# Attention with two MLPs in float32 products: the query/key high copies move from ScalarE to GpSimd, and every third two-block high copy of the transposed weights moves from ScalarE to VectorE

## Chip, core and metric

One core of a Trainium2 chip. The time is device microseconds (us) of one execution. Engines are named as the profile names them: PE is TensorE (PEld its weight loads), DVE is VectorE, ACT is ScalarE, POOL is GpSimd, SP issues the DMAs.

## What is computed

```python
scores = scale * np.matmul(q, k.transpose(0, 1, 3, 2))      # (4, 8, 576, 576), head_dim 64
thresh = np.max(scores, axis=-1, keepdims=True) - tau
scores = np.where(scores >= thresh, scores, -1000000000.0)
attn = softmax(scores)
x = np.matmul(attn, v)                                      # heads side by side: (2304, 512)
x = (silu(x @ w_gate) * (x @ w_val)) @ w_out                # first MLP, d_ff 1536
x = relu(x @ w_in) ** 2 @ w_out2                            # second MLP, d_ff 2048
```

## The kernel before

Products are made in a reduced-width float32 format (fp32r). A value that needs more width is kept as two tiles, a high copy (the value rounded to fp32r) and a low copy (the value less its high copy), and a product of two such values takes three matmuls. A **high copy** is one instruction that copies, a **low copy** one that subtracts.

**Phase 1, attention (to about 445 us).** 16 pairs of heads, four pairs in each of four batches, nine tiles of 128 query rows per pair: 144 tiles. The loop over tiles calls these steps, which the names below refer to:

- `QK` (L615): score matmuls into one of two score buffers `s`.
- `RED` (L625, DVE): the row maximum less tau. `CUT` (L633, ACT): scores below it are pushed out, into the single buffer `z`. `EXP` (L641, ACT): into one of three buffers `e`, with the row sum.
- `RCP` (L646, DVE): the reciprocal of the row sum. `NORM` (L651, POOL): `e` is scaled by it.
- `TR` (L670, PE): two tiles later, `e` is transposed in five 128-column blocks, three into one PSUM bank (the three-block half, 128x384) and two into another (the two-block half, 128x256). From tile 20 on there are only these two banks, used alternately, so each half of a tile waits until the same half of the tile before has been read out.
- `PH` (L690, ACT): the high copies of the two halves into `pt`. `PL` (L61 writing `pt`, DVE): the low copies, which read the bank again and the high copy; with the second read the bank is free for the next `TR`.
- `AV` (L716; L713 in batch 0): attention times values into `xF`, through a DMA `pt<-pt` on SP (L701) that moves a tail of 64 rows.

In batch 0 the weights are kept whole instead of split: one half is copied by ACT and the other by DVE (`ways` K and E, L53 and L55, writing `x`), and AV takes one matmul per block (L713). In batches 1 to 3 every tile is of `way` V: both high copies by ACT, both low copies by DVE.

**Preparing the next pair** (`pair_steps`, called one step at a time in the tile loop for pairs 1 to 15): the raw queries and keys, 128x576 each, get high copies into `land` (queries L560 on ACT with the scale, keys L53 on ACT), then the low copy of the queries on DVE (L566) and that of the keys on POOL (L61 writing `raw`, two halves); twelve DMAs on SP spread them over the two heads' tiles `qs`, `kh`, `kl`; POOL makes `qt` and the values' copies `vs`.

**The loader.** Until about 180 us weights for the first MLP are converted from the 64-bit words of the input, in 128x256 pieces: ACT L137, four DVE instructions (L139, L141, L145, L147), a high copy on ACT, a low copy on POOL (L61 writing `wa`, `wx`).

**The fill.** From the end of batch 0 the first MLP's first group (five of twelve d_ff blocks, L226, L271) is run for six half batches in between, as work for PE while attention waits for other engines. **Phase 2**, from 445 us, is the rest of the MLPs.

**What sets the order.** The code is written tile by tile, and each step carries a priority offset (`CFG["early"]`). A scheduler that knows the engines and a cost per instruction sets each engine's queue from that; a queue then runs strictly in order on the chip. So moving an instruction to another engine changes the order of others as well.

Of the kernel before, what the change touches and what calls it, by code (L numbers as in the profile page):

```python
# [14 lines left out]
AF = mybir.ActivationFunctionType  # L15
# [4 lines left out]
P = 128  # L20
B, H, S, D = 4, 8, 576, 64
# [46 lines left out]
def attention_moe(tc, qkv, qk0, tau, w1, w2, out, cfg):  # L68
    nc = tc.nc
    ops = Ops(nc)  # L70
# [525 lines left out]
    pt = ptp.tile([P, 10, 640], F32R, name="pt", tag="pt")  # L596
# [56 lines left out]

    WAYS = {"V": "VV", "F": "AA", "E": "AD", "K": "DA", "D": "DD"}

    def way(t):
        b, p, i = tiles[t]
        return WAYS[cfg["way"][b % len(cfg["way"])][i]]  # L660

# [18 lines left out]
    def halves(t):  # L680

        return ((st[t]["tx"], 0, 3, way(t)[0]), (st[t]["ty"], 3, 2, way(t)[1]))

    def PH(t):
        o = PTCOL[tiles[t][2]]
        for src, s0, n, how in halves(t):
            if how in "AD":
                ops.copy(how, ptf[:, s0 : s0 + n, o : o + P], src)
                continue
            nc.scalar.activation(pt[:, s0 : s0 + n, o : o + P], src, AF.Copy)  # L690

    def PL(t):
        o = PTCOL[tiles[t][2]]
# [139 lines left out]
    for i in range(NTILE + lag + 1):  # L833
# [11 lines left out]
        if 0 <= t < NTILE:  # L845
            at_(PH, t)
# [164 lines left out]
def pack(inputs):  # L1011
# [38 lines left out]


CFG = {
    "kh": "A",
    "kl": "P",
    "vh": "P",
    "vl": "P",
    "way": ("KEKKEKKEK", "VVVVVVVVV", "VVVVVVVVV", "VVVVVVVVV"),
    "lag": 2,
    "xh": "AAAA",
    "xl": "DDDD",  # L1060
    "u1": ("P", "P"),
    "u2": ("A", "D"),
    "qs": "A",
    "zs": 1,
    "wl": "PD",
    "live": (3, 2),
# [18 lines left out]
def program(arrays):  # L1085
    import concourse.bacc as bacc

    nc = bacc.Bacc("TRN2", target_bir_lowering=False, num_devices=1, dynamic_dma_scratch_size=1024)
    args = [nc.dram_tensor(n, a.shape, mybir.dt.from_np(a.dtype), kind="ExternalInput").ap() for n, a in arrays]
    out = nc.dram_tensor("out_0_dram", (NT, DM), F32, kind="ExternalOutput").ap()  # L1090
    with tile.TileContext(nc) as tc:
        attention_moe(tc, *args, out, CFG)
    return nc
# [9 lines left out]
```

## Time and profile before

| | us |
|---|---|
| median of 3 runs | 1168.59 |
| the three runs | 1168.59, 1168.98, 1165.98 |
| the profiled execution | 1168.51 |
| its span, first to last instruction | 1166.7 |
| granted TensorE clock, mean | 0.998 of full speed |

The profile page gives each engine's busy time over the span. PE is busy 97% of it, DVE 71%, ACT 57%, POOL 21%, but these are averages over phase 1, where four engines share each tile, and phase 2, where PE alone is full. A PE row's duration holds the pipeline's latency, so that rows overlap and a busy PE can still lose time: what PE loses is read better from how many matmuls it starts in a stretch.

### The profile page before, as it was taken

The numbers are of one execution on the slowest core, as the hardware profiler recorded it, in microseconds if no ns is written. First come the engines' busy times: TensorE is split into PE (matmuls) and PEld (weight loads), VectorE is DVE, ScalarE is ACT, GpSimd is POOL, SyncE is SP. The second block draws the span as 40 slices with busy tenths as digits, with TensorE's granted clock in tenths as the row PEclk, the third lists the DMA queues.
The fourth block names the chain that finished last, engine by engine and source line by source line (L and its number), as shares of the span: only waits on it lengthen the run. The fifth ranks groups of instructions, "written<-read, shape, count | busy, mean of one in ns | idle before, by whom it ended". The sixth has DMA issues, their size and how long they took to land.

```text
span 1166.7 us, 19455 instructions
## 1 busy us (share of the span) xinstructions
PE 1128.8 (97%) x6444; PEld 993.8 (85%) x6444; DVE 832.6 (71%) x2042; ACT 667.7 (57%) x1570; POOL 250.7 (21%) x397
## 2 busy tenths in 40 slices
PE   6888999999999999999999999999999999999998
PEld 5667889899999999998888888888888888888887
DVE  6988997877787773988976854478458758755433
ACT  6888988988888872554433422255455435433321
POOL 5556664656554531000000000000000000000000
PEclk9999999999999999999999999999999999999999
DMA  6775554555454510332210210002102101100111
GB/s 195 192 212 158 154 126 115 121 120 140 114 127 116 127 23 20 92 99 81 82 46 28 81 37 1 1 28 82 37 19 77 50 19 46 46 1 1 46 61 58
DMA packets 52053, 92.70 MB, mean 79 GB/s; under 512 B 8176, under 2 KB 16368, under 8 KB 51952
## 3 DMA queue, kind: packets, MB, share of 16 engines
q1 hardware_dynamic: 51808, 91.45, 28.4%
q8 instruction: 51, 0.84, 0.3%
q14 instruction: 50, 0.41, 0.1%
q10 hardware_dynamic: 144, 0.00, 0.0%
HBM read 51.91 MB, written 4.72 MB: 49 GB/s over the span
## 4 chain that ended last, share of the span: by engine, by line
PE 77%; DVE 8%; ACT 5%; DMA 4%; issue 3%; POOL 1%; SPq 0%; POOLq 0%; ACTq 0%; DVEq 0%
PE mm L226 34%; PE mm L317 17%; PE mm L271 9%; PE bank L226 5%; PE bank L670 3%; PE bank L716 3%; PE bank L271 3%; PE s L615 2%; DMA pt<-pt 2%; DVE st__101 L625 2%; DVE pt L61 2%; ACT z L633 1%; ACT e L641 1%; ACT pt L690 1%; PE bank L713 1%
## 5 line engine op out<-in xcount | busy, mean ns | idle before, releaser
L226 PE MATMUL mm<-xs,wa 128*128 128x512 f32 (+2 forms) x1152 | 226.3, 356 | 0.5 <-ACT x L53 0.5
L226 PEld LDWEIGHTS mm<-xs,wa 128*128 128x128 f32 x1152 | 193.5, 188 | 30.9 <-ACT x L53 0.7
L226 PE MATMUL mm<-xs,wb 128*128 128x512 f32 (+1 forms) x840 | 175.5, 368 | 0.0
L670 PE MATMUL bank<-ident,e 128*128 128x128 f32 x720 | 158.5, 278 | 16.8 <-DVE pt L61 5.3
L226 PEld LDWEIGHTS mm<-xs,wb 128*128 128x128 f32 x840 | 146.8, 189 | 26.3
L651 POOL TENSOR_SCALAR e<-e,r 128x576 f32<-128x576 f32 x144 | 112.8, 783 | 131.0 <-DVE r L646 89.0
L61 DVE TENSOR_TENSOR pt<-bank,pt 128x384 fp32r<-128x384 f32 x216 | 100.3, 486 | 43.1 <-ACT pt L690 41.2
L625 DVE TENSOR_SCALAR_CACHE_REDUCE st__101<-s,tau_c 128x576 bf16<-128x576 f32 x144 | 116.7, 810 | 7.7 <-PE s L615 6.7
L633 ACT ACTIVATE z<-s,thr 128x576 f32<-128x576 f32 x144 | 106.8, 741 | 25.3 <-DVE st__101 L625 19.1
L670 PEld LDWEIGHTS bank<-ident,e 128*128 128x128 f32 x720 | 94.9, 142 | 30.4 <-POOL e L651 9.3
L300 ACT ACTIVATE k_th<-mm 128x512 f32<-128x512 f32 (+1 forms) x80 | 43.7, 546 | 121.3 <-PE mm L226 120.1
L226 PE MATMUL bank<-xs_m,wa 128*128 128x288 f32 x576 | 107.6, 323 | 2.9 <-DVE xs_m L61 2.2
L641 ACT ACTIVATE e<-z 128x577 f32<-128x577 f32 x144 | 99.6, 692 | 1.7
L690 ACT ACTIVATE pt<-bank 128x384 fp32r<-128x384 f32 x216 | 87.9, 437 | 19.1 <-PE bank L670 18.2
L226 PEld LDWEIGHTS bank<-xs_m,wa 128*128 128x128 f32 x576 | 87.9, 189 | 6.4 <-DVE xs_m L61 3.6
L615 PE MATMUL s<-kh,qs 128*128 128x288 f32 x256 | 79.8, 324 | 9.3 <-DVE qs L500 5.9
L301 DVE TENSOR_TENSOR k_th<-k_th 128x512 f32<-128x512 f32 (+1 forms) x80 | 50.8, 635 | 53.1 <-ACT k_th L300 52.6
L716 PE MATMUL bank<-pt,vs 128*128 128x256 f32 (+1 forms) x432 | 84.3, 318 | 1.5 <-DMA pt<-pt 1.3
L137 ACT ACTIVATE wf<-wr 128x256 f32<-128x256 f32 x106 | 45.6, 433 | 69.6 <-DMA wr<-in_w_dram 57.9
L330 DVE TENSOR_TENSOR xF<-xF,mm 128x512 f32<-128x512 f32 x54 | 37.0, 685 | 54.7 <-PE mm L317 54.7
L615 PE MATMUL s<-kl,qs 128*128 128x288 f32 x256 | 74.5, 304 | 0.0
L716 PEld LDWEIGHTS bank<-pt,vs 128*128 128x128 f32 x432 | 66.5, 189 | 2.8 <-issue 2.4
(120 smaller groups left out, 2136.6 us busy)
## 6 DMA issues: line engine op xcount, KB each, us to landing
wr<-in_w_dram SPq DMA_DIRECT2D x106, 256.0 KB, 2.9
raw<-in_qkv_dram SPq DMA_DIRECT2D x15, 896.0 KB, 5.1
kh<-land SPq DMA_DIRECT2D x60, 144.0 KB, 2.5
kl<-raw SPq DMA_DIRECT2D x60, 144.0 KB, 2.6
xF<-in_w_dram SPq DMA_DIRECT2D x30, 256.0 KB, 3.2
kd<-kl SPq DMA_DIRECT2D x32, 144.0 KB, 2.4
out_dram<-xF SPq DMA_DIRECT2D x18, 256.0 KB, 2.0
qs<-land SPq DMA_DIRECT2D x30, 144.0 KB, 2.4
```

The source lines that it names most:

```text
L61: e.tensor_tensor(out, a, b, op=ALU.subtract)
L226: mm(pt[:, :n], w[:, a, col + c * P : col + (c + 1) * P], xs[:, b, c, :], start=(i == 0), stop=(i == len(TERMS) - 1),)
L271: mm(pt[:, :n], w[:, a, 2 * DM + m * P : 2 * DM + (m + 1) * P], u[:, b, :], start=(k == 0), stop=(k == last),)
L317: mm(pt, u[:, b, s * P : (s + 1) * P], w[:, a, DM : 2 * DM], start=(k == 0), stop=(k == last),)
L615: mm(sp[:, cols], l, r[:, cols], start=(n_ == 0), stop=(n_ == len(pairs) - 1),)
L625: red = nc.vector.tensor_scalar(st_, st[t]["s"][:, :S], scalar1=tau_c, scalar2=None, op0=ALU.subtract, op1=ALU.max, accum_out=th)
L633: nc.scalar.activation(z[:, :S], st[t]["s"][:, :S], AF.Prelu, bias=st[t]["thr"], scale=-1.0, alpha=1 / SLOPE)
L641: ex = nc.scalar.activation(e, st[t]["z"], AF.Exp, scale=-SLOPE, accum_out=sum_)
L651: nc.gpsimd.tensor_scalar(e, e, scalar1=r, scalar2=1.0, op0=ALU.mult, op1=ALU.mult)
L670: mm(dst[:, j], e[:, c0 : c0 + P], ident, is_transpose=True, start=(j == 0), stop=(j == len(cols) - 1),)
L690: nc.scalar.activation(pt[:, s0 : s0 + n, o : o + P], src, AF.Copy)
L716: mm(o[:, :n], hd["vs"][:, SLOT[k % 5], :], pt[:, k, lo : lo + n], start=(k == 0), stop=(k == 9))
```

## The change

`CFG["kh"]` and `CFG["qs"]` go from A to P: in `pair_steps` both high copies into `land` (L560 and L53 before) are made by POOL, for the 15 pairs that go through it. A new way H is VV with the difference that `PH` makes the two-block half's high copy on DVE; in batches 1 to 3 the tiles 2, 5 and 8 of each pair's nine are of way H, 36 of 108 tiles. Low copies, DMAs and the arithmetic stay.

```diff
-    WAYS = {"V": "VV", "F": "AA", "E": "AD", "K": "DA", "D": "DD"}
+    WAYS = {"V": "VV", "H": "VH", "F": "AA", "E": "AD", "K": "DA", "D": "DD"}
...
             if how in "AD":
                 ops.copy(how, ptf[:, s0 : s0 + n, o : o + P], src)
                 continue
-            nc.scalar.activation(pt[:, s0 : s0 + n, o : o + P], src, AF.Copy)
+            ops.copy("D" if how == "H" else "A", pt[:, s0 : s0 + n, o : o + P], src)
...
 CFG = {
-    "kh": "A",
+    "kh": "P",
...
-    "way": ("KEKKEKKEK", "VVVVVVVVV", "VVVVVVVVV", "VVVVVVVVV"),
+    "way": ("KEKKEKKEK", "VVHVVHVVH", "VVHVVHVVH", "VVHVVHVVH"),
...
-    "qs": "A",
+    "qs": "P",
```

In the built program POOL has 30 more instructions that write `land` (15 of L562, 15 of L57), ACT 30 fewer and 36 fewer that write `pt` (216 to 180), and DVE 36 new ones (L55 CAST writing `pt`). The scheduler has moved others with them. Three places follow, before and then after in each.

The queue of POOL at the end of batch 0, where pair 4 is prepared; `e0_97` and `e1_98` with `r30` and `r31` are the NORMs of tiles 30 and 31. Before:

```order
L651 TENSOR_SCALAR e0_97<-e0_97,r30_1023 128x576
L61 TENSOR_TENSOR vs8_1156<-raw4_982,vs8_1156 128x5x64
L57 TENSOR_SCALAR vs9_1231<-raw4_982 128x5x64
L61 TENSOR_TENSOR wa_69<-xF_64,wa_69 128x256
L61 TENSOR_TENSOR vs9_1231<-raw4_982,vs9_1231 128x5x64
L61 TENSOR_TENSOR raw4_982<-raw4_982,land4_984 128x288 x2
L57 TENSOR_SCALAR qt02_117<-qs8_1123 64x64
L61 TENSOR_TENSOR wx_73<-wf2_80,wx_73 128x256
L651 TENSOR_SCALAR e1_98<-e1_98,r31_1052 128x576
```

After:

```order
L651 TENSOR_SCALAR e0_97<-e0_97,r30_1023 128x576
L562 TENSOR_SCALAR land4_984<-raw4_982,qscale_59 128x576
L57 TENSOR_SCALAR land4_984<-raw4_982 128x576
L57 TENSOR_SCALAR vs8_1156<-raw4_982 128x5x64
L61 TENSOR_TENSOR raw4_982<-raw4_982,land4_984 128x288 x2
L61 TENSOR_TENSOR vs8_1156<-raw4_982,vs8_1156 128x5x64
L57 TENSOR_SCALAR vs9_1231<-raw4_982 128x5x64
L61 TENSOR_TENSOR wa_69<-xF_64,wa_69 128x256
L61 TENSOR_TENSOR vs9_1231<-raw4_982,vs9_1231 128x5x64
L61 TENSOR_TENSOR wa_69<-xF_64,wa_69 128x256
L651 TENSOR_SCALAR e1_98<-e1_98,r31_1052 128x576
```

The two `land` copies stand in the block between the two NORMs, which goes from eight instructions to ten; a `qt` copy and a piece of `wx` have moved behind it, and the first `vs8` copy and a piece of `wa` into it.

The queue of DVE in batch 1, pair 1, while the loader still runs, from the RED of tile 52 (`thr52`); `pt` written from `bank0` and `bank1` are the two PLs of a tile, `xs_m01` splits the next fill's input. Before:

```order
L625 TENSOR_SCALAR st__101,thr52_1926<-s0_108,tau_c_60 128x576
L728 TENSOR_TENSOR xF_64<-xF_64,bank3_87 64x256
L646 RECIPROCAL r51_1940<-sum51_1887 128x1
L61 TENSOR_TENSOR pt_131<-bank0_84,pt_131 128x3x128
L256 SCALAR_TENSOR_TENSOR m00_4_th_1813<-m00_4_th_1813,bank2_86 128x288
L61 TENSOR_TENSOR pt_131<-bank1_85,pt_131 128x2x128
L61 TENSOR_TENSOR xs_m01_1948<-xF_64,xs_m01_1948 128x288
```

After:

```order
L625 TENSOR_SCALAR st__101,thr52_1926<-s0_108,tau_c_60 128x576
L147 SCALAR_TENSOR_TENSOR xF_64<-xF_64 128x256
L728 TENSOR_TENSOR xF_64<-xF_64,bank3_87 64x256
L256 SCALAR_TENSOR_TENSOR m00_4_th_1813<-m00_4_th_1813,bank2_86 128x288
L141 TENSOR_SCALAR xF_64<-xF_64 128x256
L566 SCALAR_TENSOR_TENSOR raw6_1727<-raw6_1727,qscale_59,land6_1729 128x576
L145 SCALAR_TENSOR_TENSOR xF_64<-xF_64 128x256
L61 TENSOR_TENSOR xs_m01_1948<-xF_64,xs_m01_1948 128x288 x2
L646 RECIPROCAL r51_1940<-sum51_1887 128x1
L61 TENSOR_TENSOR xs_m01_1948<-xF_64,xs_m01_1948 128x288 x2
L61 TENSOR_TENSOR pt_131<-bank0_84,pt_131 128x3x128
L61 TENSOR_TENSOR pt_131<-bank1_85,pt_131 128x2x128
```

The tile's two PLs stood third and fifth behind the RED; now they stand behind ten other instructions, among them L566, three of the loader and all four of `xs_m01`.

The queue of DVE in batch 2, after the loader's end, from the RED of tile 106. Before:

```order
L625 TENSOR_SCALAR st__101,thr106_4213<-s0_108,tau_c_60 128x576
L728 TENSOR_TENSOR xF_64<-xF_64,bank3_87 64x256
L646 RECIPROCAL r105_4224<-sum105_4179 128x1
L61 TENSOR_TENSOR pt_131<-bank0_84,pt_131 128x3x128
L61 TENSOR_TENSOR pt_131<-bank1_85,pt_131 128x2x128
L625 TENSOR_SCALAR st__101,thr107_4265<-s1_109,tau_c_60 128x576
L646 RECIPROCAL r106_4275<-sum106_4218 128x1
L61 TENSOR_TENSOR pt_131<-bank0_84,pt_131 128x3x128
L61 TENSOR_TENSOR pt_131<-bank1_85,pt_131 128x2x128
L625 TENSOR_SCALAR st__101,thr108_4300<-s0_108,tau_c_60 128x576
```

After:

```order
L625 TENSOR_SCALAR st__101,thr106_4213<-s0_108,tau_c_60 128x576
L728 TENSOR_TENSOR xF_64<-xF_64,bank3_87 64x256
L646 RECIPROCAL r105_4224<-sum105_4179 128x1
L61 TENSOR_TENSOR pt_131<-bank0_84,pt_131 128x3x128
L61 TENSOR_TENSOR pt_131<-bank1_85,pt_131 128x2x128
L646 RECIPROCAL r106_4275<-sum106_4218 128x1
L625 TENSOR_SCALAR st__101,thr107_4265<-s1_109,tau_c_60 128x576
L55 CAST pt_131<-bank1_85 128x2x128
L61 TENSOR_TENSOR pt_131<-bank0_84,pt_131 128x3x128
L61 TENSOR_TENSOR pt_131<-bank1_85,pt_131 128x2x128
L625 TENSOR_SCALAR st__101,thr108_4300<-s0_108,tau_c_60 128x576
```

The CAST of an H tile stands directly in front of that tile's two PLs, and the RCP has changed places with the RED.

## Rows read from the trace of the kernel before

**Rows 1.** Windows by stage: length, busy us and instructions per engine, clock, DMA.

```profile
8.00:60.00 52.00, 43.72 (x233) 35.83 (x232) 44.48 (x120) 44.54 (x108) 29.13 (x46) 1.00 0.72 195
60.00:128.00 68.00, 59.53 (x359) 50.01 (x358) 59.43 (x162) 60.95 (x151) 43.20 (x62) 0.97 0.63 174
128.00:180.00 52.00, 47.80 (x348) 44.65 (x348) 48.99 (x127) 45.43 (x116) 33.35 (x51) 1.00 0.53 134
180.00:300.00 120.00, 115.97 (x861) 109.99 (x860) 94.55 (x258) 103.50 (x260) 66.58 (x107) 1.00 0.52 124
300.00:445.00 145.00, 142.74 (x1083) 138.76 (x1082) 109.77 (x298) 121.67 (x306) 70.01 (x110) 1.00 0.41 97
445.00:1166.70 721.70, 716.91 (x3565) 612.58 (x3564) 472.57 (x1073) 288.72 (x632) 4.65 (x8) 1.00 0.14 46
```

**Rows 2.** Windows, the fullest 20 us of batch 3: columns as in Rows 1.

```profile
420.00:440.00 20.00, 19.95 (x155) 19.71 (x155) 12.04 (x34) 14.17 (x37) 5.24 (x8) 1.00 0.06 13
```

**Rows 3.** Waits, 180 to 445 us: who waited for whom, us, times, longest.

```profile
POOL e L651 <- DVE r L646: 54.8, 38, 3.0
DVE pt L61 <- ACT pt L690: 39.6, 67, 1.2
...
PE bank L670 <- DVE pt L61: 2.3, 6, 0.7
```

**Rows 4.** Timeline around 157 us: start, us, engine, line, operation, idle before.

```profile
154.00 1.57 POOL L61 TENSOR_TENSOR raw<-raw,land 128x288 fp32r<-128x288 f32 x2
154.52 1.34 DVE L145 SCALAR_TENSOR_TENSOR xF<-xF 128x256 int32<-128x256 int32 x1
155.78 0.84 DVE L139 TENSOR_SCALAR wf<-wf 128x256 f32<-128x256 f32 x1
157.60 0.30 PE L670 MATMUL bank<-ident,e 128*128 128x128 f32 x1 [1.26 <-DVE pt L61]
```

**Rows 5.** Timeline around 229 us: columns as in Rows 4.

```profile
228.30 0.50 ACT L690 ACTIVATE pt<-bank 128x384 fp32r<-128x384 f32 x1
228.82 0.22 ACT L53 ACTIVATE xF<-bank 64x64 f32<-64x64 f32 x1
229.05 0.38 ACT L690 ACTIVATE pt<-bank 128x256 fp32r<-128x256 f32 x1
229.63 0.52 PE L670 MATMUL bank<-ident,e 128*128 128x128 f32 x3 [0.65 <-DVE pt L61]
```

**Rows 6.** Tile raw: duration ns min/median/max, first and last start us, forms.

```profile
L514 POOL TENSOR_SCALAR qs<-raw,qscale x1: 744/744/744, 7.3 to 7.3; 128x576 fp32r<-128x576 f32 x1
L57 POOL TENSOR_SCALAR vs<-raw x24: 452/458/1044, 91.7 to 407.4; 128x320 fp32r<-128x320 f32 x24
L560 ACT ACTIVATE land<-raw,qscale x15: 760/777/820, 16.5 to 390.5; 128x576 fp32r<-128x576 f32 x15
L566 DVE SCALAR_TENSOR_TENSOR raw<-raw,qscale,land x15: 796/820/1435, 17.3 to 391.4; 128x576 fp32r<-128x576 f32 x15
L53 ACT ACTIVATE land<-raw x15: 665/682/705, 17.8 to 391.2; 128x576 fp32r<-128x576 f32 x15
```

**Rows 7.** Groups by form, ACT and DVE, 180 to 445 us: busy, mean ns, idle before.

```profile
L690 ACT ACTIVATE pt<-bank 128x256 fp32r<-128x256 f32 x89 | 34.3, 386 | 0.8 <-PE bank L670 0.7
L61 DVE TENSOR_TENSOR pt<-bank,pt 128x384 fp32r<-128x384 f32 x88 | 48.8, 554 | 33.6 <-ACT pt L690 32.4
```

**Rows 8.** Groups by form, DVE, 8 to 128 us: columns as in Rows 7.

```profile
L55 DVE COPY x<-bank 128x256 f32<-128x256 f32 x12 | 5.0, 420 | 2.6 <-PE bank L670 2.5
```

**Rows 9.** Groups by form, DVE L145, 128 to 180 us: columns as in Rows 7.

```profile
L145 DVE SCALAR_TENSOR_TENSOR xF<-xF 128x256 int32<-128x256 int32 x5 | 3.5, 709 | 0.0
```

**Rows 10.** Groups by form, DVE L145, 445 us to the end: columns as in Rows 7.

```profile
L145 DVE SCALAR_TENSOR_TENSOR wf<-wr,wf 128x256 int32<-128x256 int32 x106 | 44.6, 421 | 1.5
```

**Rows 11.** Timeline of POOL and PE at the end of batch 0: columns as in Rows 4.

```profile
97.24 1.97 POOL L61 TENSOR_TENSOR raw<-raw,land 128x288 fp32r<-128x288 f32 x2
...
100.10 0.74 POOL L651 TENSOR_SCALAR e<-e,r 128x576 f32<-128x576 f32 x1
100.89 0.76 PE L670 MATMUL bank<-ident,e 128*128 128x128 f32 x5 [1.68 <-POOL e L651]
```

## The prediction, made before the changed kernel ran

> **What bounds the kernel now.** I read the windows by stage first. From 445 us on PE is busy 716.9 of 721.7 us and ACT 288.7: nothing that the change touches is left to be late there, so that only the first 445 us can move, and they move the end one for one [rows 1]. In them I ask how much PE loses, because the matmuls are the same in both kernels. Busy time hides it, so I count starts: in the fullest stretch PE starts 155 matmuls in 20 us, 129 ns each [rows 2]. At that rate the 348 of 128 to 180 us need 44.9 of 52 us, the 861 of 180 to 300 us need 111.1 of 120, and the 1083 of 300 to 445 us need 139.7 of 145 [rows 1]. PE loses some 7.1, 8.9 and 5.3 us there, 21 us in all. (The mix of matmuls differs a little between stretches; I give each loss an error of 1 us.) Before 128 us there is no fill to run and PE is not the bound at all: ACT is busy 105.5 and DVE 103.9 of 120 us.
>
> Then the waits, to see who makes PE lose that. The two-bank turn of the transposes is the place: PE waits for DVE's low copy, which waits for ACT's high copy, 39.6 us in 67 waits after 180 us [rows 3]. Two samples tell the stages apart. Near 157 us PE sits idle 1.26 us for a low copy that DVE reaches late because the loader's instructions stand ahead of it; one of them took 1.34 us, with POOL subtracting beside it [rows 4]. That is DVE's lateness: it is busy 49.0 of 52 us there [rows 1]. Near 229 us PE sits idle 0.65 us, and ACT has been copying without a break, with two pieces of `xF` work between and behind the two high copies [rows 5]. That is ACT's lateness.
>
> **What the change takes and adds.** ACT loses 15 query copies of 777 ns and 15 key copies of 682 ns [rows 6], 21.9 us, and 36 two-block copies of 386 ns [rows 7], 13.9 us: 35.8 us in all. DVE gains 36 copies out of PSUM of that shape. No row of before has it writing `pt`, but the same engine copies the same 128x256 out of a bank into `x` in 420 ns [rows 8]: 15.1 us. POOL gains 30 copies of 128x576. The one such copy with the scale took 744 ns, and 458 ns for 320 columns would make at most 824 for 576 [rows 6]. I take 770 ns, nearest the first because it is the same shape: 23.1 us, with 22.3 and 24.7 as ends.
>
> *Up to 128 us.* Five pairs are prepared there, so ACT loses 5 x 1.46 = 7.3 us. If ACT alone set the pace the whole of it would come off, and if DVE did, nothing; they are equally busy, and each tile passes through both in turn, so I take a quarter, -1.8 us. Against it stand two prices on POOL's side. First, an instruction of DVE that reads SBUF takes longer beside POOL: the loader's L145 took 709 ns at 128 to 180 us and 421 after POOL had fallen silent [rows 9, 10], L566 between 796 and 1435 [rows 6]. POOL, busy 72.3 of 120 us, gets 7.7 us more, about a tenth. If a loader instruction is stretched by 0.29 us where POOL works six tenths of the time, a tenth more of POOL's time stretches some 100 of them by 0.03 to 0.05 us: 3 to 5 us of DVE work at most, of which I put 0.8 on the path, since only part of DVE's queue is waited for. Second, POOL's queue is in order, and the two copies stand ahead of a NORM at the end of batch 0. There the block is already late: two subtractions of 1.97 us, then NORM, and PE idle 1.68 us for it [rows 11]. Two copies are 1.54 us more in that block, less a `qt` and a `wx` that have left it, plus a `vs` and a `wa` that have come in. I take +0.5, with 0 and +1.5 as ends. Sum -0.5, between -5 (most of ACT's time comes off) and +3.
>
> *128 to 180 us.* Six H tiles fall here: 6 x 0.42 = 2.5 us on an engine that has 3 us to spare in 52 [rows 1], so that it would be busy 99%. ACT's relief (2.9 + 2.3 us) is not what this stage waits for. The new order adds to it: in the second place shown, the two low copies of a tile stand behind the loader, L566 and all of `xs_m01`, some 4 us of DVE later than before, though the order gives PE a dozen more fill matmuls there first (about 1.6 us). I take +2, between 0 (the casts replace waits for ACT) and +4.
>
> *180 to 445 us.* ACT is busy 225.2 of 265 us, 85%; eight pairs and 29 casts take 11.7 + 11.2 = 22.9 us off, and it falls to 76%. DVE goes from 204.3 us to 216.5, 77% to 82%. The casts have a cover: DVE sits idle 33.6 us ahead of the three-block low copy [rows 7], and in the third place shown a cast stands just there, so that ACT copies one half while DVE copies the other. Without that cover they cost up to 12.2 us. POOL waits 54.8 us for reciprocals before its NORMs [rows 3], and no wait of PE for POOL is among the large ones here, so 12.3 us more on POOL cost nothing; without that slack each pair would pay up to 1.5 us. Of the 14.2 us that PE loses here, part is the wait for `pt<-pt` transfers and for the fill's own split, which ACT's relief hardly touches. I call half of it, 7 us, ACT's lateness, and take half of that off, -3.5, since only one two-block copy in three is moved and the three-block one, on which DVE waits most, stays on ACT. New lateness of DVE gives back 1. Sum -2.5, between -7 and +3.
>
> In all -0.5 + 2 - 2.5 = -1.0 us. The profiled execution took 1168.51 us, 1.8 more than its span and the same as the median to 0.1 us, so the forecast is 1167.5 us.
>
> [...]
>
> **The rivals.** *Relief goes through.* If ACT's order is what makes nearly all of the low copies late, the 7 us after 180 us go entirely, and batch 0 gives 3 of its 7.3 us; the start of batch 1 gives 1 back. Then -9, and 1159.5 us. For it: ACT is the fuller engine after 180 us, and 32.4 of the 33.6 us that DVE idles before the three-block low copy end with ACT [rows 7]. Against it: PE's plain idle waits for the low copy are only 2.3 us there [rows 3].
>
> *DVE becomes the bound (slower).* A cast has to wait for its transposes on PE, and everything behind it in DVE's queue waits too: the RED that starts a later tile, and the low copies. It decides if the casts stand where DVE was not idle: of 15.1 us, the 2.5 at 128 to 180 us in full and 5 of the 12.2 after, plus the 4 us later low copies of the second place shown at half, less 1.5 us of relief: +8, and 1176.5 us.
>
> *POOL holds DVE (slower).* If each of the 14 new copies up to 180 us holds a DVE instruction for half its length, DVE gets 14 x 0.39 = 5.4 us later where it is the fuller or the equal engine, and the casts' +2 come on top, with -2.5 after 180 us: +5, and 1173.5 us. [...]
>
> *It doesn't do what it says.* The built order rules that out: the 30 copies stand on POOL and the 36 on DVE, and ACT has none of them.
>
> **How the numbers follow.** 0.3%, 3.5 us, is about what a measurement of this kernel can tell from no change. The forecast, within it: 0.41. Relief goes through, faster by more: 0.34, which takes in cases between 1159.5 and 1165. The two slower ones: DVE 0.17, POOL's hold 0.08, 0.25 together. The stages' ends sum to far more than any likely case, so the range goes by the cases: from a little above the relief rival's time, 1160, to 1175 us, which leaves out about 1 in 10 on either side.
>
> **What would show it.** Right: PE's matmuls between 128 and 180 us fewer than 348, and more between 180 and 445 us; DVE's waits for ACT's high copy well below 39.6 us; ACT near 76% there. Wrong: batch 0's end (the first RED of batch 1) moved by more than 3 us; casts with long waits for TR, or NORMs that PE waits for after 128 us; L566 and the loader's rows longer in the mean by 0.2 us or more, which would be POOL's hold; a cast in `pt` far from 420 ns. The forecast falls if ACT's lateness is more than half of PE's loss, or if the reordered queues lose more than the loads say, since I priced orders at two places and not at all 144 tiles.

## The result, and the profile after

The changed kernel takes 1179.09 us (median of 6 runs, 1173.55 to 1181.69), the kernel before beside it 1167.99 (1165.73 to 1169.07): a ratio of 1.0094, with a 95% interval of 1.0067 to 1.0121. It is 11 us slower, and lies above the range of 1160 to 1175 us. The profiled execution after took 1180.1 us, 1.8 more than its span.

The first question is where the 11 us arise. The matmuls are the same, so I cut both traces at the same work: the first RED of pair 4 (where batch 1 begins), that of pair 7, and the last RED of all. The windows of the kernel before, cut there (us, then busy time and instructions of PE, PE's loads, DVE, ACT and POOL, PE's granted clock, DMA share, GB/s):

```profile
8.00:107.20 99.20, 84.21 (x462) 68.88 (x462) 84.74 (x232) 86.14 (x211) 59.28 (x88) 0.98 0.68 185
107.20:191.80 84.60, 78.56 (x563) 72.76 (x562) 76.26 (x201) 74.87 (x187) 51.68 (x77) 1.00 0.54 139
191.80:427.80 236.00, 230.06 (x1727) 221.07 (x1727) 187.53 (x511) 204.61 (x512) 129.30 (x204) 1.00 0.49 117
```

The same three pieces of work after the change:

```profile
8.00:113.30 105.30, 86.35 (x463) 70.23 (x462) 84.39 (x229) 82.50 (x201) 65.20 (x93) 0.94 0.64 171
113.30:204.60 91.30, 79.42 (x561) 73.88 (x560) 78.40 (x212) 69.97 (x176) 57.62 (x85) 0.98 0.51 132
204.60:440.00 235.40, 228.53 (x1728) 221.30 (x1729) 195.17 (x536) 191.32 (x467) 140.55 (x219) 1.00 0.49 117
```

PE has the same matmuls in both, some 462, 562 and 1727 (a row or two of a piece falls on the other side of a cut). The first piece is 6.1 us longer, the second 6.7, the third 0.6 shorter: everything is lost while batch 0 and the first three pairs of batch 1 run, and nothing after. Of the 12.8 us lost, 3.0 are PE's busy time (84.21 to 86.35 and 78.56 to 79.42, for the same matmuls), and 9.8 are idle time of PE.

Two kinds of place show what PE waits for. The first is pair 1, while its rows are still coming in. Before, GpSimd ran its two NORMs and VectorE the reciprocal that the second of them needs, while ScalarE waited for the rows. From the timeline of the kernel before, engine by engine (start, us, engine, line, operation, and in brackets the idle time before it and what ended it):

```profile
13.50 1.56 POOL L651 TENSOR_SCALAR e<-e,r 128x576 f32<-128x576 f32 x2
...
14.06 0.16 DVE L646 RECIPROCAL r<-sum 128x1 f32<-128x1 f32 x1 [0.71 <-ACT e L641]
...
16.52 0.77 ACT L560 ACTIVATE land<-raw,qscale 128x576 fp32r<-128x576 f32 x1 [2.50 <-DMA raw<-in_qkv_dram]
...
17.98 0.61 PE L615 MATMUL s<-kh,qs 128*128 128x288 f32 x1 [1.71 <-ACT z L633]
```

The same place after the change:

```profile
13.48 0.75 POOL L651 TENSOR_SCALAR e<-e,r 128x576 f32<-128x576 f32 x1
...
16.65 0.75 POOL L562 TENSOR_SCALAR land<-raw,qscale 128x576 fp32r<-128x576 f32 x1 [2.42 <-DMA raw<-in_qkv_dram]
...
17.43 1.21 DVE L566 SCALAR_TENSOR_TENSOR raw<-raw,qscale,land 128x576 fp32r<-128x576 f32 x1 [4.09 <-POOL land L562]
18.12 1.97 POOL L61 TENSOR_TENSOR raw<-raw,land 128x288 fp32r<-128x288 f32 x2
...
18.57 0.15 DVE L646 RECIPROCAL r<-sum 128x1 f32<-128x1 f32 x1
...
20.07 0.78 POOL L651 TENSOR_SCALAR e<-e,r 128x576 f32<-128x576 f32 x1
...
20.90 0.90 PE L670 MATMUL bank<-ident,e 128*128 128x128 f32 x3 [3.26 <-POOL e L651]
...
21.61 0.42 ACT L53 ACTIVATE wa<-xF 128x256 fp32r<-128x256 f32 x1 [4.95 <-DVE xF L147]
```

The query copy waits 2.42 us at the head of GpSimd's queue for the rows, and L566 on VectorE waits 4.09 us for that copy. Behind L566 stands the reciprocal, now at 18.57 instead of 14.06 us, and behind the copies and subtractions on GpSimd the NORM that needs it: it starts at 20.07 us, and PE idles 3.26 us for it. Behind the reciprocal stands the loader's work, and ScalarE waits 4.95 us for that. The wait for the rows is no longer than before, 2.42 us against 2.50; it stands where more is queued behind it. It was not free before either: the CUT behind ScalarE's wait kept PE idle for 1.71 us. What the change costs here is the difference: pair 1's first RED comes at 34.4 instead of 31.2 us.

The second comes twice, at the end of batch 0 and near 131 us. Here the loader's low copies (`wa` on L61), which free the buffers of the next weight pieces, come behind the pair's block in GpSimd's queue. At the end of batch 0:

```profile
101.20 0.72 POOL L61 TENSOR_TENSOR wa<-xF,wa 128x256 fp32r<-128x256 f32 x1
...
101.95 0.43 ACT L137 ACTIVATE xF<-xF 128x256 f32<-128x256 f32 x1 [4.23 <-POOL wa L61]
102.29 0.37 ACT L53 ACTIVATE x<-bank 128x256 f32<-128x256 f32 x1
...
102.71 0.44 PE L670 MATMUL bank<-ident,e 128*128 128x128 f32 x2 [2.58 <-ACT x L53]
```

ScalarE stands 4.23 us at L137, the first step of a new weight piece, until the low copy of an old one has freed its buffer. Behind L137 stands the copy that empties a bank of transposes, and PE idles 2.58 us for that. Near 131 us it is the high copy of a tile's three-block half that stands behind L137; VectorE's low copy waits for it, and PE for that low copy:

```profile
130.24 1.40 POOL L61 TENSOR_TENSOR wa<-xF,wa 128x256 fp32r<-128x256 f32 x2
131.00 0.43 ACT L137 ACTIVATE xF<-xF 128x256 f32<-128x256 f32 x1 [2.98 <-POOL wa L61]
...
132.02 0.48 ACT L53 ACTIVATE pt<-bank 128x384 fp32r<-128x384 f32 x1
...
132.52 0.56 DVE L61 TENSOR_TENSOR pt<-bank,pt 128x384 fp32r<-128x384 f32 x1 [3.29 <-ACT pt L53]
...
133.23 0.45 PE L670 MATMUL bank<-ident,e 128*128 128x128 f32 x1 [3.16 <-DVE pt L61]
```

ScalarE, the engine that the change relieves, is stopped by the work that the change put on GpSimd. Summed over the first two pieces of work, the waits of ScalarE (waited for: us in total, times, longest) after the change have

```profile
ACT xF L137 <- POOL wa L61: 8.3, 4, 4.2
...
ACT wf L137 <- POOL wa L61: 2.6, 2, 1.3
```

and the list of ScalarE's waits in the kernel before names no low copy. PE's own waits over the same two pieces, before:

```profile
PE bank L670 <- ACT x L53: 4.6, 6, 1.8
PE bank L670 <- DVE pt L61: 3.0, 6, 1.3
PE bank L670 <- POOL e L651: 2.9, 3, 1.7
```

and after:

```profile
PE bank L670 <- DVE pt L61: 6.7, 6, 3.2
PE bank L670 <- POOL e L651: 6.0, 4, 3.3
PE bank L670 <- ACT x L53: 4.6, 6, 2.6
```

The waits for NORMs grow by 3.1 us and those for VectorE's low copies by 3.7. Those for ScalarE's bank copies stay at 4.6 us: the long one at the end of batch 0 stands in place of shorter ones.

### The profile page after: what moved, and what is told of

Read it like the earlier page. It is cut to its first block, busy times and chain, and to the rows that moved or that the text cites. A ratio compares the mean times of both kernels' runs of the same rounds, so it can differ in the third digit from the quotient of the medians.

```text
span 1178.3 us, 19364 instructions
## 1 busy us (share of the span) xinstructions
PE 1129.7 (96%) x6444; PEld 996.0 (85%) x6444; DVE 842.9 (72%) x2078; ACT 646.3 (55%) x1504; POOL 274.0 (23%) x427
## 4 chain that ended last, share of the span: by engine, by line
PE 78%; DVE 6%; ACT 4%; DMA 4%; issue 3%; POOL 2%; SPq 1%; POOLq 0%; ACTq 0%; DVEq 0%
PE mm L226 34%; PE mm L317 17%; PE mm L271 9%; PE bank L226 5%; PE bank L670 4%; PE bank L716 3%; PE s L615 3%; PE bank L271 3%; DMA pt<-pt 1%; DMA raw<-in_qkv_dram 1%; DVE st__101 L625 1%; ACT z L633 1%; ACT e L641 1%; PE bank L713 1%; DVE pt L61 1%
## 5 line engine op out<-in xcount | busy, mean ns | idle before, releaser
L226 PE MATMUL mm<-xs,wa 128*128 128x512 f32 (+2 forms) x1152 | 226.3, 356 | 0.5 <-ACT x L53 0.5
L226 PEld LDWEIGHTS mm<-xs,wa 128*128 128x128 f32 x1152 | 193.5, 188 | 30.9 <-ACT x L53 0.7
L226 PE MATMUL mm<-xs,wb 128*128 128x512 f32 (+1 forms) x840 | 175.5, 368 | 0.0
L226 PEld LDWEIGHTS mm<-xs,wb 128*128 128x128 f32 x840 | 146.8, 188 | 26.4
L651 POOL TENSOR_SCALAR e<-e,r 128x576 f32<-128x576 f32 x144 | 113.3, 787 | 117.7 <-DVE r L646 68.2
L61 DVE TENSOR_TENSOR pt<-bank,pt 128x384 fp32r<-128x384 f32 (+1 forms) x216 | 99.8, 484 | 39.3 <-ACT pt L53 38.2
L226 PE MATMUL bank<-xs_m,wa 128*128 128x288 f32 x576 | 105.8, 321 | 3.9 <-DVE xs_m L61 2.1
L226 PEld LDWEIGHTS bank<-xs_m,wa 128*128 128x128 f32 x576 | 87.2, 189 | 7.0 <-DVE xs_m L61 3.4
L53 ACT ACTIVATE pt<-bank 128x384 fp32r<-128x384 f32 (+1 forms) x180 | 76.2, 446 | 30.5 <-PE bank L670 27.2
L615 PE MATMUL s<-kh,qs 128*128 128x288 f32 x256 | 80.8, 329 | 11.1 <-DVE qs L500 5.9
L716 PE MATMUL bank<-pt,vs 128*128 128x256 f32 (+1 forms) x432 | 84.7, 320 | 4.1 <-DMA pt<-pt 4.0
L137 ACT ACTIVATE wf<-wr 128x256 f32<-128x256 f32 x106 | 45.7, 434 | 69.7 <-DMA wr<-in_w_dram 56.6
L330 DVE TENSOR_TENSOR xF<-xF,mm 128x512 f32<-128x512 f32 x54 | 37.0, 685 | 54.5 <-PE mm L317 54.5
L615 PE MATMUL s<-kl,qs 128*128 128x288 f32 x256 | 74.6, 304 | 0.0
```

Of the source, the lines that this page charges most:

```text
L53: nc.scalar.activation(out, in_, AF.Copy)
L61: e.tensor_tensor(out, a, b, op=ALU.subtract)
L226: mm(pt[:, :n], w[:, a, col + c * P : col + (c + 1) * P], xs[:, b, c, :], start=(i == 0), stop=(i == len(TERMS) - 1),)
L615: mm(sp[:, cols], l, r[:, cols], start=(n_ == 0), stop=(n_ == len(pairs) - 1),)
L651: nc.gpsimd.tensor_scalar(e, e, scalar1=r, scalar2=1.0, op0=ALU.mult, op1=ALU.mult)
L716: mm(o[:, :n], hd["vs"][:, SLOT[k % 5], :], pt[:, k, lo : lo + n], start=(k == 0), stop=(k == 9))
```

## Experiments

The theory, "POOL's queue": the copies of queries and keys lose the time by what stands behind them in GpSimd's in-order queue while weight pieces are still loaded (to about 180 us); the casts of VectorE lose nothing, and the relief of ScalarE gives nothing. The rivals: the casts on a full VectorE, and GpSimd holding VectorE.

All twelve kernels, with the kernel before run beside each group. "Pieces" are the lengths of the three pieces of work in the one trace of each. Executions of one kernel spread by up to 8.1 us (the changed kernel, 1173.55 to 1181.69), so a piece says where time went in one execution, and the medians say how much:

| kernel | median, us | before, us | ratio (95%) | pieces, us |
|---|---|---|---|---|
| before | | | | 99.2, 84.6, 236.0 |
| after | 1179.09 | 1167.99 | 1.0067 to 1.0121 | 105.3, 91.3, 235.4 |
| copies alone | 1179.9 | 1168.19 | 1.0067 to 1.0131 | 104.3, 93.0, 234.7 |
| casts alone | 1168.6 | 1168.19 | 0.9994 to 1.0020 | 97.5, 85.2, 237.4 |
| copies, pairs 1 to 7 | 1179.96 | 1168.19 | 1.0067 to 1.0120 | 104.3, 91.5, 236.5 |
| copies, pairs 8 to 15 | 1169.18 | 1168.19 | 0.9998 to 1.0022 | 97.9, 85.8, 235.6 |
| copies, not pair 1 | 1177.06 | 1168.38 | 1.0047 to 1.0090 | 101.6, 88.7, 236.9 |
| extra work on GpSimd | 1174.24 | 1168.38 | 1.0031 to 1.0061 | 101.4, 88.6, 234.4 |
| key copies alone | 1172.82 | 1168.38 | 1.0020 to 1.0048 | 99.5, 87.3, 237.0 |
| copies, low copies earlier | 1173.38 | 1168.38 | 1.0030 to 1.0063 | 102.5, 87.2, 236.6 |
| low copies earlier, alone | 1168.52 | 1168.71 | 0.9985 to 1.0012 | 99.0, 85.4, 235.0 |
| low copies earlier, not pair 1 | 1170.54 | 1168.71 | 1.0007 to 1.0032 | 101.3, 84.7, 235.5 |
| late copies, casts, low copies earlier | 1169.33 | 1168.71 | 0.9990 to 1.0021 | 98.7, 86.0, 236.5 |
| casts in every tile | 1177.55 | 1168.71 | 1.0053 to 1.0109 | 97.6, 92.7, 237.5 |

One rival runs through all of them: the scheduler sets every queue anew, so that few edits change one thing only. By the order of the rows in the traces (names without buffer numbers), the copies alone put 134 of VectorE's 2042 instructions at another place, the casts alone 97. The casts alone lose nothing by that; what the new order costs beside the copies, no kernel here tests by itself.

**The two parts, one at a time.** Copies alone, from the changed kernel:

```diff
-    "way": ("KEKKEKKEK", "VVHVVHVVH", "VVHVVHVVH", "VVHVVHVVH"),
+    "way": ("KEKKEKKEK", "VVVVVVVVV", "VVVVVVVVV", "VVVVVVVVV"),
```

> Only the copies of queries and keys go to GpSimd; no high copy of a two-block half goes to VectorE. Theory 'POOL's queue' (the two copies, standing in GpSimd's in-order queue while it also has the weight pieces' low copies and the NORMs to do, are the whole loss of about 11 us, and it arises before 190 us): 1176 to 1181, with the first RED of the seventh and eighth pair about 10 us late. Rival 'casts on a full VectorE' (the casts of tiles 38 to 62 cost the 6 us that are lost between 107 and 177 us): 1172 to 1175, with the lag at the eighth pair no larger than at the end of batch 0 (6 us).

Casts alone, from the changed kernel:

```diff
-    "kh": "P",
+    "kh": "A",
...
-    "qs": "P",
+    "qs": "A",
```

> Only the high copies of the two-block half go to VectorE; queries and keys stay on ScalarE. Theory 'POOL's queue': 1165 to 1169, within 0.3% of before. Rival 'casts on a full VectorE': 1172 to 1175, all of it lost between 128 and 180 us, with casts standing ahead of a low copy that TensorE waits for.

The copies alone lose 11.7 us, the whole; the casts alone 0.4, which is not told apart from nothing. The rival of the casts is out, for 36 of them.

**Early or late.** From the copies alone, the copies go to GpSimd for some pairs only. For pairs 1 to 7:

```diff
-        if cfg["qs"] == "A":
+        if cfg["qs"] == "A" or p > 7:
...
-        ops.copy(cfg["kh"], kh, k)
+        ops.copy("A" if p > 7 else cfg["kh"], kh, k)
```

> The copies go to GpSimd only for pairs 1 to 7, which are prepared while the weight pieces still come; later pairs and all casts are as before. Theory 'POOL's queue': all of the loss, 1176 to 1181. Rival 'GpSimd holds VectorE whenever it works on these copies' (the loss would come evenly over all 15 pairs): under half of it, 1170 to 1173.

The other kernel has `p <= 7` in both lines.

> The copies go to GpSimd only for pairs 8 to 15, prepared after the last weight piece. Theory 'POOL's queue': 1164 to 1168, as before or a little faster, since ScalarE is relieved by 13 us and nothing queues behind the copies on GpSimd. Rival 'GpSimd holds VectorE': 1172 to 1175, half of the loss.

The first seven pairs cost 11.8 us, the last eight 1.0, with an interval that reaches below zero (and to 2.6 us above); that is 1.2 us above the theory's band and 2.8 below the rival's. GpSimd does eight pairs' copies there beside the same VectorE and next to nothing is lost, so GpSimd's load as such does not explain the 11 us. A hold on VectorE that costs evenly is out as well; one that costs only early, where VectorE is fuller, is taken up below. What differs early is the loader, and the rows of pair 1.

**Pair 1.** From the copies alone:

```diff
-        if cfg["qs"] == "A":
+        if cfg["qs"] == "A" or p == 1:
...
-        ops.copy(cfg["kh"], kh, k)
+        ops.copy("A" if p == 1 else cfg["kh"], kh, k)
```

> The copies of all pairs but pair 1 go to GpSimd; pair 1, which is prepared while its rows still come in (12 to 21 us), keeps them on ScalarE. Theory 'POOL's queue': the first stall goes, where a NORM stood behind a copy that waited for the rows, so the lag of 3.2 us at pair 1 and part of the half clock behind it: 1174 to 1177. Rival 'the first stall is made up anyway': 1179 to 1181, the lag at pair 7 as large as with the copies of all pairs.

It gives back 3.0 of 11.7 us (8.7 are left), 0.1 us above the theory's band. By itself that is not clear of noise, since the intervals of the two losses (7.8 to 15.3 and 5.5 to 10.5 us) overlap; the same edit is seen once more below, beside the other cure. In its trace the second piece gains more (4.3 us) than the first (2.7), so not all of the gain of that execution is the stall at pair 1. That stall is gone; both NORMs run ahead of the wait again, as in the kernel before:

```profile
13.63 1.56 POOL L651 TENSOR_SCALAR e<-e,r 128x576 f32<-128x576 f32 x2
```

**GpSimd's time, without the data.** From the kernel before: ScalarE keeps the copies, and GpSimd copies both finished tiles into a piece of `x2` that is not used yet.

```diff
+    pad = x2[0][1][:, 2:4, LAST - HS :]
...
         ops.copy(cfg["kh"], kh, k)
+        for x_ in (qh, kh) if p <= 7 else ():
+            ops.copy("P", pad, x_.bitcast(F32).rearrange("p (a c) -> p a c", a=2))
```

> ScalarE makes the copies of queries and keys as before; for pairs 1 to 7 GpSimd copies the two finished tiles once more into a scratch tile that nobody reads, so its queue is as full as in the changed kernel but no copy waits there for a transfer and nothing waits for a GpSimd copy. Theory A, 'GpSimd's time' (2.1 us more per pair ahead of the weight pieces' low copies are enough): 1173 to 1179. Theory B, 'what waits in the queue' (the copies stand in the queue before their rows are there, and the steps behind them start from GpSimd instead of ScalarE): 1166 to 1171.

5.9 us: theory A's band, yet only half of 11.7. GpSimd's bare time, ahead of what is queued behind it, is worth one half of the loss. This is the cleanest of the tests: no row of VectorE or ScalarE has changed its place, and three of GpSimd's beside the 14 new ones (766 ns in the mean, the real copies 752). The other half belongs to what this kernel leaves as it was: nothing waits for a GpSimd copy, no NORM stands behind a wait for the rows (at pair 1 GpSimd waits 2.42 us for ScalarE's copy, after both NORMs), and the queues of VectorE and ScalarE keep their order. How the other half divides among these was not tested.

**The keys alone.** From the copies alone:

```diff
-    "qs": "P",
+    "qs": "A",
```

> Only the copy of the keys goes to GpSimd, that of the queries stays on ScalarE. Theory A, 'GpSimd's time': about half of the loss, 1172 to 1176. Theory B, 'what waits in the queue': nearly all of it, 1176 to 1180, since one copy that waits for the rows holds the queue as two do.

4.4 us, less than half of the loss: theory A again. Pair 1 begins 2.0 us late here too (33.2 us for 31.2), but pair 2 begins early (54.5 for 55.8): with one copy the first stall is made up, and the first piece ends 0.3 us longer than before.

**The low copies earlier.** From the copies alone, the loader's low copies (`LP`) get a higher priority:

```diff
-        ... "FP": -100, "PL": 30, ...
+        ... "FP": -100, "LP": 200, "PL": 30, ...
...
-        ... "LP": -100,
+        ... "LP": 100,
```

> Copies of queries and keys on GpSimd for all pairs, no casts, and the low copies of the weight pieces get a higher priority in the order, so that in a few places they stand ahead of a pair's copies, NORMs or value copies. Theory 'POOL's queue': some of the loss between 97 and 177 us comes back, 1173 to 1178. Rival 'the weight pieces don't matter': 1179 to 1182.

6.7 of 11.7 us come back (5.0 are left). The place near 131 us in the changed kernel comes at 126 us here, and its stall is gone: a low copy stands between the two halves of the keys' subtraction, and neither L137 nor the high copy behind it waits for GpSimd.

```profile
124.83 1.25 POOL L61 TENSOR_TENSOR wa<-xF,wa 128x256 fp32r<-128x256 f32 x1
...
126.11 0.44 ACT L137 ACTIVATE xF<-xF 128x256 f32<-128x256 f32 x1
...
126.93 0.49 ACT L53 ACTIVATE pt<-bank 128x384 fp32r<-128x384 f32 x1 [0.37 <-PE bank L670]
```

At the end of batch 0 it is not gone. ScalarE still waits there for a low copy, 3.19 us at 98.98 us, and PE waits as long as in the changed kernel:

```profile
99.74 0.44 PE L670 MATMUL bank<-ident,e 128*128 128x128 f32 x2 [2.60 <-ACT x L53]
```

L137's total over the first two pieces falls from 8.4 us with the copies alone to

```profile
ACT xF L137 <- POOL wa L61: 4.8, 2, 3.2
```

and PE's waits for VectorE's low copies, 7.5 us with the copies alone, are 0.4 us. In these traces the second piece gains 5.8 us and the first 1.8: what came back came from batch 1 in the main, not from the end of batch 0.

**Is that a gain of its own?** The same two edits, on the kernel before. They move one row there, on GpSimd.

```diff
+        ... "LP": 200, ...
...
-        ... "LP": -100,
+        ... "LP": 100,
```

> The kernel before with nothing but the higher priority of the weight pieces' low copies, which moves one row of one engine there. Theory 'POOL's queue' (the low copies are late only where the pairs' copies stand ahead of them): 1166 to 1170, as before. Rival 'the higher priority is a gain of its own': 1160 to 1164, and then what it gave back beside the copies says nothing on them.

0.2 us faster than before, which is nothing: the higher priority is no gain of its own and only undoes what the copies did. With the copies it moves 28 rows of GpSimd and also 60 of VectorE and 30 of ScalarE, so the 6.7 us are those of the new order as a whole. That they come from the low copies is argued from the stall near 131 us, not shown by itself. The 6.7 us do speak against a hold: GpSimd makes the same copies beside the same early VectorE in both kernels.

**Both cures.** From the copies alone, pair 1 on ScalarE and the higher priority:

```diff
+        if cfg["qs"] == "A" or p == 1:
...
+        ops.copy("A" if p == 1 else cfg["kh"], kh, k)
...
+        ... "LP": 200, ...
...
+        ... "LP": 100,
```

> Copies on GpSimd for pairs 2 to 15, pair 1 on ScalarE, and the higher priority of the low copies; no casts. If the two causes are separate, their gifts add: of the loss of 11.7 us the first took 3.0 and the second 6.7, so 2 us are left, 1169 to 1172. If both removed the same stall: 1172 to 1175.

1.8 us are left, where 2.0 would be if the two add. Beside the higher priority, pair 1's edit is worth 3.2 us (5.0 to 1.8), as it was 3.0 without it. The two gains are separate, then: some 3 us with the copies of pair 1, and 6.7 with the order in which the loader's low copies stand. Of the 1.8 us that are left the trace shows a source: at the end of batch 0 ScalarE still waits 3.80 us for a low copy, and PE 2.83 us for the bank copy behind it, so this place was cured by neither edit.

**Where the gain went.** From the changed kernel: copies on GpSimd for pairs 8 to 15 only, casts as they are, the higher priority:

```diff
+        if cfg["qs"] == "A" or p <= 7:
...
+        ops.copy("A" if p <= 7 else cfg["kh"], kh, k)
...
+        ... "LP": 200, ...
...
+        ... "LP": 100,
```

> The whole change, but with the copies of pairs 1 to 7 left on ScalarE, and the higher priority of the low copies. Theory 'after the last weight piece TensorE is the bound, so relief of ScalarE is worth nothing there': 1166 to 1170. Rival 'casts and late copies together give what neither gives alone' (ScalarE at 76% of 180 to 445 us): 1158 to 1164.

0.6 us above before, not told apart from it. With all that slowed it gone, the relief of ScalarE that is left (the casts and the late copies) is worth nothing that shows. None of these kernels beats the kernel before.

**How far the cover of the casts goes.** From the casts alone, 108 of them:

```diff
-    "way": ("KEKKEKKEK", "VVHVVHVVH", "VVHVVHVVH", "VVHVVHVVH"),
+    "way": ("KEKKEKKEK", "HHHHHHHHH", "HHHHHHHHH", "HHHHHHHHH"),
```

> Queries and keys on ScalarE; VectorE makes the high copy of the two-block half in all 108 tiles of batches 1 to 3 instead of 36: 72 more casts of 420 ns, 30 us of VectorE, of which about 20 us come after 180 us, where its share rises from 78 to about 90%. Theory 'idle time covers the casts': 1167 to 1171. Rival 'VectorE becomes the bound': 1174 to 1185, with TensorE waiting for low copies and RED coming later from pair to pair after 180 us.

8.8 us slower, but not where the rival had it: the second piece is 8.1 us longer than before, the third 1.5. These two pieces in this kernel:

```profile
105.60:198.30 92.70, 82.71 (x569) 76.91 (x567) 83.84 (x225) 69.45 (x164) 52.10 (x78) 0.94 0.49 125
198.30:435.80 237.50, 229.71 (x1727) 222.75 (x1726) 213.54 (x591) 187.26 (x430) 129.56 (x203) 0.99 0.49 116
```

VectorE is busy 214 of 237 us in the late piece and PE still 230. In the early one, with the loader's work on VectorE too, VectorE has 7.6 us more to do and the piece is 8.1 us longer; its share stays at 90%. PE's clock has a part in it: at 0.94 PE is busy 4.2 us longer for the same work.

## Why the prediction was wrong, point by point

**What bounds the kernel.** That only the first 445 us can move holds. That PE "is not the bound at all" before 128 us holds too (though not that there is no fill to run: its first row, L226, starts at 117.39 us), and it is there, and in the next 60 us, that the loss lies. The prediction then looked at ACT and DVE as the two that set the pace there and asked only at one place what POOL's order does.

**Up to 128 us, -0.5 (from -5 to +3): the step that failed.** The term "POOL's queue in order" was put at +0.5, at most +1.5, from the one block at the end of batch 0 [rows 11], as 1.54 us of time ahead of one NORM. The first piece of work lost 6.1 us. Three things were left out. *The copies wait.* The row of ScalarE's 2.50 us wait for the rows of pair 1 was in the trace of before; moving the instruction moves the wait, in front of another queue, and that was not costed (some 3 us). *What is queued behind is more than NORMs.* The loader's low copies stand there, ScalarE's L137 waits for their buffers, and the copies that empty PE's banks stand behind L137 (6.7 us came back over both pieces when the low copies were put earlier). *It happens at four places*, near 49, 102, 131 and 148 us, not once. The relief of ScalarE, -1.8, came to nothing: in the first two pieces ScalarE stood 10.9 us for POOL's low copies instead.

The traces show the queues in order. On VectorE, the reciprocal's input came at the same time in both kernels (ScalarE's EXP starts at 13.26 and 13.25 us), and yet it ran 4.5 us later behind an L566 that waited 4.09 us, and nothing passed it. On ScalarE, the bank copy at 102.29 us had its transposes by 98.41 us and ran behind the L137 that waited 4.23 us. On GpSimd, the rows from 95.78 to 103.46 us come as the queue shown for the end of batch 0 has them.

**128 to 180 us, +2 (0 to +4).** The casts, which were to cost it, cost 0.4 us in all; their second piece is 85.2 us long against 84.6. They took 420 ns as the row of the `x` copies said [rows 8]:

```profile
L55 DVE CAST pt<-bank 128x256 fp32r<-128x256 f32 x25 | 10.5, 420 | 2.6 <-PE bank L670 2.3
```

The second piece lost 6.7 us instead through the copies (93.0 us with the copies alone). The sum's other reason did show: in the second place of the order, the RED of tile 53 follows that of tile 52 after 8.2 us instead of 3.9, and PE stands 1.21 us for `xs_m` in between. But the copies alone have that too (7.2 us), so it is the copies' doing. The sign was right, the cause was not.

**180 to 445 us, -2.5 (-7 to +3).** No gain came. "Half of what PE loses is ScalarE's lateness" was the choice that failed; the list of waits had 2.3 us of PE for the low copy [rows 3], and that was the figure to go by. The waits of PE over the third piece, before (5.0 us in all):

```profile
PE bank L670 <- DVE pt L61: 2.3, 6, 0.7
PE bank L226 <- DVE xs_m L61: 1.1, 4, 0.4
PE bank L716 <- DMA pt<-pt: 1.1, 3, 0.5
PE s L615 <- ACT z L633: 0.5, 1, 0.5
```

and after:

```profile
PE bank L716 <- DMA pt<-pt: 2.4, 4, 1.1
PE bank L670 <- DVE pt L61: 1.7, 3, 1.0
```

The wait for the low copy shrinks by 0.6 us and that for the `pt<-pt` transfers grows by 1.3. ScalarE's time went into ScalarE's own waiting for PE, as its three-block copy shows, before and after (busy, mean ns | idle before, what ended it):

```profile
L690 ACT ACTIVATE pt<-bank 128x384 fp32r<-128x384 f32 x80 | 39.0, 487 | 11.2 <-PE bank L670 10.9
```

```profile
L53 ACT ACTIVATE pt<-bank 128x384 fp32r<-128x384 f32 x80 | 39.0, 488 | 17.5 <-PE bank L670 15.1 <-DVE st__101 L625 1.4
```

PE is busy 230 of 236 us there; a relief of the engines beside it found nothing to give.

**The rivals.** *Relief goes through* (1159.5 us) is out: with the losses gone, 0.6 us above before. *DVE becomes the bound* is out for 36 casts; with 108 the second piece grows by about what VectorE has more to do. *POOL holds DVE* is out as a main cause: beside GpSimd's 14 early copies L145 went from 514 to 594 ns in the mean and `xs_m` on L61 from 471 to 658, but L147, L141 and L139 went down by 34, 31 and 18 ns; with the copies alone VectorE's busy time over the first two pieces is 161.9 us, 0.9 more than before. And the same early copies cost 5.0 us with the low copies earlier, and all but pair 1's then 1.8. That a copy holds VectorE for half its length, 0.39 us each, was the author's estimate, and no run shows it. What the trace of before shows is uneven: each L145 of the loader that took over 0.43 us had a GpSimd row beside it (the longest took 1.34 us), others beside GpSimd took 0.40 to 0.43 us, as those alone did, and all 144 RED, which read a score buffer, took 0.79 to 0.82 us. The rows of the first two pieces, before and after:

```profile
L145 DVE SCALAR_TENSOR_TENSOR xF<-xF 128x256 int32<-128x256 int32 x20 | 10.3, 514 | 0.2
L566 DVE SCALAR_TENSOR_TENSOR raw<-raw,qscale,land 128x576 fp32r<-128x576 f32 x7 | 6.9, 984 | 1.4 <-ACT land L560 1.2
```

```profile
L145 DVE SCALAR_TENSOR_TENSOR xF<-xF 128x256 int32<-128x256 int32 x20 | 11.9, 594 | 0.1
L566 DVE SCALAR_TENSOR_TENSOR raw<-raw,qscale,land 128x576 fp32r<-128x576 f32 x7 | 7.4, 1062 | 4.9 <-POOL land L562 4.9
```

L566 costs 0.5 us more in length and 3.5 more in waiting for the copy: the wait is what the copies brought, more than a hold.

**What would show it.** The sign named first under "wrong" came: the first RED of batch 1 moved from 107.2 to 113.3 us. Of the signs called right, two misled. PE's matmuls at 128 to 180 us did fall, to 307, but because all work was late. After 180 us they stayed at 1944, as before. ScalarE's share fell to 81% of the third piece and not to 76%: the rows of one engine overlap (L560 took 0.77 us from 16.52, and the next began at 17.20; on PE, a row of L615 took 0.30 us from 97.58, and the next began at 97.72), so an instruction that goes takes off less busy time than its row is long.

The size of the POOL copies was right: 805 and 699 ns in the mean over the first seven pairs, for 770 taken, and it was never the point.

## What to carry to other kernels

Moving an instruction to a less busy engine moves its waits as well (here 2.50 us on ScalarE, then 2.42 on GpSimd): look up what it waited for where it stands, and who is queued behind it where it goes. A busy share of 60% says nothing on that; GpSimd had the time and not the order. And before relieving an engine, add up what the bound engine waits for in that stage: here it was 5 us of 236, and no kernel gained from it.

## What the runs showed of the hardware

PE's clock had a part in the loss. Beside and after the stalls above, PE was granted half of full speed for a part of the stretches that follow: the granted clock was 0.50 from 20 to 26 us and from 106 to 108 us. Windows of the kernel after:

```profile
20.00:40.00 20.00, 17.57 (x88) 14.28 (x88) 15.37 (x45) 15.44 (x38) 11.34 (x18) 0.83 0.63 158
...
100.00:120.00 20.00, 13.97 (x73) 11.02 (x72) 14.84 (x40) 15.17 (x39) 12.93 (x20) 0.91 0.56 141
```

Before, one stretch of 20 us up to 200 us fell below 1.00 (80 to 100 us, 0.91); after, four do. PE idled 3.26 us up to 20.90 us, and 2.58 us within the second of these. A pair of the same matmuls, at a granted clock of 0.50 and of 1.00:

```profile
22.66 1.06 PE L713 MATMUL bank<-x 128*128 128x256 f32 x2
...
97.16 0.60 PE L713 MATMUL bank<-x 128*128 128x256 f32 x2
```

What it costs is read from the windows of the three pieces: 3.0 us more busy time for the same matmuls, a quarter of what the two early pieces lost. That this part goes when some of the stalls go is seen in the kernel with the low copies earlier, where PE is busy 83.81 and 79.35 us at 0.97 and 0.98 of the clock, instead of 86.49 and 81.68 us at 0.93 and 0.96 with the copies alone; no run changed the clock alone.

What stays open is how the time that the earlier low copies gave back divides between them and the other rows whose places moved with them, and what the new order of VectorE's and ScalarE's queues costs by itself beside the copies.
